# Linear attention and top-1 experts on one core: attention steps regrouped by array shape, scores as 64x64 products, first loads by half heads, early places for four chunks, a fixed load order

## The chip, the cores and the metric

The kernel runs on one core of a Trainium2 chip. The core has a matrix engine (TensorE, "PE" in the profile, its weight loads "PEld"), a vector engine (VectorE, "DVE"), a scalar engine (ScalarE, "ACT"), a general one (GpSimd, "POOL") and one that mostly issues transfers (SyncE, "SP"). They run side by side, each through its own queue in order, and wait for each other through semaphores. Transfers between the device memory (DRAM) and the on-chip memory (SBUF) run on 16 DMA engines; they are issued from the queues of SP, ACT or POOL. PE's products land in PSUM, eight banks of 128 partitions x 512 numbers of 4 bytes. All data are 32-bit floats.

The metric is the device time of one execution in microseconds (us). Before the change the median of 10 runs is 477.11 us (476.78 to 479.06).

## The reference: what is computed

Two parts in a row. First linear attention with a decay: 4 batches, 8 heads, 768 positions, 64 numbers a head. In blocks of 64 positions (the kernel uses blocks of 128, which gives the same sums):

```python
intra = np.einsum('bhic,bhjc->bhij', qb, kb) * Dmask[None]
intra = np.einsum('bhij,bhjd->bhid', intra, vb)
inter = np.einsum('bhid,bhde->bhie', qb * lam_pow[None], kv_state)
out[:, :, sl] = intra + inter
kv_state = lam_block[None, :, None, None] * kv_state + np.einsum('bhsd,bhse->bhde', kb_dec, vb)
```

`Dmask[i, j]` is lam to the power i - j for j up to i, zero beyond; lam is one number a head. Then each of the 3072 output rows of 512 numbers (4 x 768 tokens) goes through one of 8 experts, the one with the highest gate logit:

```python
expert_idx = np.argmax(logits, axis=1)          # logits = x @ w_gate
h = np.maximum(xe @ w1[e], 0.0)                 # 512 -> 1024, for the rows xe of expert e
out[mask] = gate_w[mask, None] * (h @ w2[e])    # 1024 -> 512
```

## The kernel before, in words

**Attention steps.** The positions are cut into 6 chunks of 128 (n), the batches taken in 2 pairs (b): 12 steps, numbered 0 to 11 below, in the list `order` (L699). PE's work of a step is written out by hand, and `pin` (L204) keeps each of its instructions in program order. The other engines' instructions are placed by a scheduler: it takes those that are ready in its own model of time, earlier lines first. Within a step, and for the pair two batches of one chunk:

- `turn_q` and `turn_k` (L216, L228) transpose q and k of the *next* step on PE in two halves of four heads (s = 0, 1), four 128x128 transposes each. ACT copies the results to SBUF as qT and kT, DVE writes qsT, which is q times a decay, and POOL writes kd, which is k times a decay (L238, two buffers).
- `attend_states` (L265) multiplies qsT with the state `st`: 16 products in two groups of 8 ("ways"), which write other halves of the output banks 6 and 7. Between the two an ACT copy of a few numbers (`fence`, L280) makes the second way wait for the first.
- `grow` (L296) makes the state's growth, 32 products kd x v into bank 4. `update` (L308) adds it on DVE to the decayed state, which POOL has put into `sd` (L316).
- `attend` (L282) makes 32 products of v with the masked scores `mt`, into banks 6 and 7.
- `to_sbuf` (L290) copies these two banks on ACT to xT.
- `score` (L243) makes the next step's scores: 32 products of 64x128 (64 rows of the array, 128 columns, 128 wide) into banks 0 to 3, and multiplies them on DVE with the decay mask, giving mt (L254).
- `leave` (L668) and `rows` (L320), in the next step, turn xT back to rows on PE (banks 4 to 7, with the gate's logits in 8 further columns). ACT copies the rows to x and the logits to lg, and issues the transfer of x to `xs` in DRAM.

PE's shapes in a step are 128x128 (leave, turns), 64x64 (states), 128x64 (grow, attend), 64x64 (states) and 64x128 (scores): five, the next step's leave closing the circle.

**Routing.** When a group of chunks is complete, `choose` (L338) finds on DVE each token's expert and its running counts. A step later `put` (L370) makes the token's place in its expert's list: a product with a triangular matrix (`rank`, bank 5), four small DVE operations, and one indirect transfer from POOL for each chunk. A group is the 4 chunks of one n for n = 0 to 3, and two chunks after that (L641). The group (4, [0, 1]) is called `early`: after it `start_early` (L685) reads how many tokens expert 0 has so far, fetches its first 256 rows (pass "0a"), and later tokens of expert 0 are placed behind them.

**Experts.** Nine passes ("0a", "0b" and one for each other expert), in order of their counts. A pass gathers its rows, transposes them (`turn`, L460), makes the hidden layer (`hidden`, L470, or in seven products for eight, `hidden_fast`), the outputs, and scatters them. The hidden layer of "0a" is begun while the last places are still being made (L778).

**Loads.** `load` (L89) fetches q, k and v of a pair of batches, 512 KB each, with three buffers for each of the three. Entering the next step issues the load for two steps beyond it. The first pair comes in halves by batch, k's through ACT's queue; lam comes behind q on SP's queue, and the gate weights come on ACT's in four transfers (L123). The scheduler may swap loads on SP's queue. The weights of expert 0 (two of 2 MB) are issued from step 9's `enter` (L651).

## Time and profile before

| what | value |
|---|---|
| median of 10 runs | 477.11 us |
| the profiled execution, its time | 477.9 us |
| its span, first to last instruction | 476.1 us |
| granted PE clock, mean | 0.996 |
| PE / PEld busy | 457.8 / 383.7 us |
| DVE / ACT / POOL busy | 224.4 / 126.9 / 247.7 us |
| DMA moved | 72.84 MB, mean 153 GB/s |
| one attention step (51.17 to 60.98) | 9.81 us |
| one attention step with `rank` (60.98 to 71.16) | 10.18 us |
| attention ends, last state products | 128.32 us |
| hidden layer of "0a" ends | 146.91 us |

Read it so: the span is the profiled execution of all the work, and what lies around it adds 1.8 us to give that execution's own time. PE is busy nearly all of it, but the ends of its products are modelled, so its busy time does not tell whether the products were as close as they could be; the starts in the timeline do. The attention part is the first 128 us, and up to 119 us the DMA engines are busy in nine tenths or more of the time as well. After 136 us PE's timeline shows one dense run of expert work up to the end. "L248" is line 248 of the kernel; a row's last bracket says how long the engine had been idle before it and what ended that.

### The profile page before, as it was taken

To read this page: it belongs to the slowest core of one execution; us is meant where nothing else is said; L and a number is where in the kernel's file an instruction comes from. 1 tells how busy PE (TensorE), PEld (TensorE's weight loads), DVE (VectorE), ACT (ScalarE), POOL (GpSimd) and SP (SyncE) were. 2 spreads that over 40 slices of the span, in tenths; PEclk is the share of its full clock that TensorE was granted. 3 is DMA by queue.
4 is the path that set the end of the run, shared out by engine and by line. 5 is a ranking of instruction groups with operands and counts; after the bars stand their busy time and mean duration, and the time that the engine had idled before them with its cause. 6 is when DMAs were issued, how large, how long until landed. Compare 5 with 4: busy or idle time off the path is not lost.

```text
span 476.1 us, 8695 instructions
## 1 busy us (share of the span) xinstructions
PE 457.8 (96%) x3468; PEld 383.7 (81%) x3468; DVE 224.4 (47%) x525; ACT 126.9 (27%) x323; POOL 247.7 (52%) x189
## 2 busy tenths in 40 slices
PE   4899999999999999999999999999999999999994
PEld 3789999998785677957994898699699689779973
DVE  2657758585540134462345437434534623753421
ACT  3364445554320111212121122113112212211310
POOL 5423644524335829849807951991794497711001
PEclk9999999999999999999999999999999999999998
DMA  9999999998219556060606153351633615001001
GB/s 173 238 244 269 228 235 233 281 271 271 90 48 344 149 201 237 24 248 29 220 1 243 48 202 103 140 202 44 244 121 122 241 35 209 0 19 44 1 17 51
DMA packets 99857, 72.84 MB, mean 153 GB/s; under 512 B 81227, under 2 KB 81231, under 8 KB 99809
## 3 DMA queue, kind: packets, MB, share of 16 engines
q1 hardware_dynamic: 88688, 51.97, 39.6%
q0 software_dynamic: 5008, 13.41, 7.8%
q10 hardware_dynamic: 6112, 6.83, 4.7%
q8 instruction: 29, 0.48, 0.4%
q14 instruction: 20, 0.16, 0.1%
HBM read 59.13 MB, written 13.40 MB: 152 GB/s over the span
## 4 chain that ended last, share of the span: by engine, by line
PE 91%; DMA 3%; SPq 2%; DVE 1%; ACT 1%; ACTq 0%; issue 0%; POOLq 0%; POOL 0%
PE p L551 28%; PE p L579 18%; PE po L609 16%; PE ph L475 5%; PE sp L248 4%; PE op L284 4%; PE tp L465 3%; PE tx L326 2%; PE op L272 2%; PE cp L301 2%; PE tx L328 2%; DMA k_in<-in_k_dram 2%; PE tk L213 2%; PE tq L213 2%; SPq L96 2%; DMA back<-in_moe_w_gate_dram 1%
## 5 line engine op out<-in xcount | busy, mean ns | idle before, releaser
L609 PE MATMUL po<-w2t,hT 128*128 128x512 f32 (+2 forms) x224 | 81.1, 597 | 0.0
L436 POOL DMA_INDIRECT xg<-xs,list x24 | 26.0, 1084 | 75.7 <-PE tp L465 70.2
L609 PEld LDWEIGHTS po<-w2t,hT 128*128 128x128 f32 (+2 forms) x224 | 31.6, 169 | 37.5 <-issue 37.2
L562 ACT ACTIVATE hT<-hT 128x384 f32<-128x384 f32 (+2 forms) x56 | 30.2, 538 | 89.8 <-DVE hT L560 89.8
L442 POOL DMA_INDIRECT out_dram<-o,list x24 | 23.7, 990 | 52.0 <-DVE o L615 28.9
L390 POOL DMA_INDIRECT slots<-entry,slot_i x24 | 23.7, 986 | 38.2 <-DVE slot_i L388 14.1
L551 PE MATMUL p<-xgT,w1t 128*128 128x192 f32 (+2 forms) x224 | 42.8, 334 | 0.0
L551 PEld LDWEIGHTS p<-xgT,w1t 128*128 128x128 f32 x224 | 38.7, 190 | 1.1 <-issue 0.8
L238 POOL TENSOR_TENSOR kd<-k_in,kdec 128x512 f32<-128x512 f32 x20 | 20.5, 1044 | 26.5 <-PE cp L301 14.8
L254 DVE TENSOR_TENSOR mt<-sp,decay 128x512 f32<-128x512 f32 x48 | 29.8, 682 | 7.2 <-PE sp L248 7.1
L591 DVE SCALAR_TENSOR_TENSOR o<-p,list,o 128x256 f32<-128x256 f32 x28 | 13.5, 484 | 32.9 <-PE p L579 17.0
L579 PE MATMUL p<-w2t,hT 128*128 128x256 f32 x112 | 26.8, 382 | 0.0
L579 PEld LDWEIGHTS p<-w2t,hT 128*128 128x128 f32 x112 | 21.0, 190 | 6.9 <-issue 4.4
L248 PE MATMUL sp<-qT,kT 64*128 64x128 f32 x384 | 25.1, 281 | 0.0
L248 PEld LDWEIGHTS sp<-qT,kT 64*128 64x128 f32 x384 | 22.8, 191 | 2.2 <-issue 1.9
L284 PE MATMUL op<-mt,v_in 128*64 128x128 f32 x384 | 23.6, 274 | 0.7 <-ACT fence L280 0.7
L475 PE MATMUL ph<-xgT,w1t 128*128 128x256 f32 (+1 forms) x128 | 23.9, 342 | 0.0
L560 DVE TENSOR_TENSOR hT<-p,u_qsT 128x384 f32<-128x384 f32 (+2 forms) x28 | 16.1, 575 | 16.5 <-PE p L551 16.5
L213 PE MATMUL tq<-ident,q_in 128*128 128x128 f32 x96 | 15.4, 286 | 7.5 <-DMA q_in<-in_q_dram 7.5
L284 PEld LDWEIGHTS op<-mt,v_in 128*64 128x64 f32 x384 | 20.7, 137 | 1.5 <-ACT fence L280 1.2
L488 DVE TENSOR_TENSOR u_kT<-p,u_qT 128x384 f32<-128x384 f32 (+2 forms) x14 | 8.1, 577 | 29.3 <-PE p L551 29.3
L293 ACT COPY xT<-op 128x512 f32<-128x512 f32 x24 | 12.9, 589 | 33.6 <-PE op L272 29.8
(162 smaller groups left out, 960.9 us busy)
## 6 DMA issues: line engine op xcount, KB each, us to landing
w1t<-in_moe_w_dram SPq DMA_DIRECT2D x8, 2048.0 KB, 7.9
w2t<-in_moe_w_dram SPq DMA_DIRECT2D x8, 2048.0 KB, 8.9
xs<-x ACTq DMA_DIRECT2D x24, 256.0 KB, 4.3
q_in<-in_q_dram SPq DMA_DIRECT2D x11, 512.0 KB, 8.3
k_in<-in_k_dram SPq DMA_DIRECT2D x11, 512.0 KB, 8.4
v_in<-in_v_dram SPq DMA_DIRECT2D x11, 512.0 KB, 8.8
q_in<-in_q_dram SPq DMA_DIRECT2D x2, 256.0 KB, 3.9
k_in<-in_k_dram ACTq DMA_DIRECT2D x2, 256.0 KB, 5.5
```

What stands on the lines that cost most here:

```text
L213: pin(nc.tensor.transpose(t[:, i, b, :], src[:, b, h:h + 2, :], ident))
L248: pin(nc.tensor.matmul(sp[u][:, i, b, :], lhsT=m.kT[s][halves[u], i, b, :], rhs=m.qT[s][halves[u], i, b, :], start=(i == 0 and b == 0), st ...
L254: nc.vector.tensor_mul(mt[:, u], sp[u], decay[:, u, s * HP // 2:(s + 1) * HP // 2].unsqueeze(2).to_broadcast(shp))
L284: pin(nc.tensor.matmul(out_at(m, b, u, hp), lhsT=m.v[:, b, 2 * hp + u, :], rhs=m.mt[hp // 2][:, u, hp % 2, b, :], start=(m.n == 0 and hp = ...
L390: put = nc.gpsimd.indirect_dma_start(out=slots, out_offset=bass.IndirectOffsetOnAxis(ap=slot_i[:, i:i + 1], axis=0), in_=entry[:, n, b, :] ...
L436: nc.gpsimd.indirect_dma_start(out=dst, out_offset=None, in_=xs[:rows, :], in_offset=bass.IndirectOffsetOnAxis(ap=idx, axis=0))
L442: put = nc.gpsimd.indirect_dma_start(out=out, out_offset=bass.IndirectOffsetOnAxis(ap=idx, axis=0), in_=src, in_offset=None, bounds_check= ...
L475: nc.tensor.matmul(ph, lhsT=w1t[:, dc, fc * P:(fc + 1) * P], rhs=m.xgT[:, dc, :], start=(dc == 0), stop=(dc == DC - 1))
L551: nc.tensor.matmul(p[:, i, :], lhsT=lhs[:, dc, (c + i) * P:(c + i + 1) * P], rhs=rhs[:, dc, :], start=(dc == 0), stop=(dc == DH - 1))
L562: nc.scalar.activation(outs[i][k], outs[i][k], ACT.Relu)
L579: nc.tensor.matmul(p, lhsT=lhs[:, fc, :], rhs=rhs[:, fc, :], start=(fc == 0), stop=(fc == FC // 2 - 1))
L609: nc.tensor.matmul(po[part], lhsT=m.hT[:, fc, t * P:t * P + w], rhs=w2t[:, fc, :], start=(i < k), stop=(i >= FC - k), skip_group_check=True)
```

## The change

- `score` makes 64 products of 64x64 instead of 32 of 64x128: the columns (keys) are split in halves. The masks move to a function of their own, `mask`.
- A step's order becomes: for each half s, turns of the next step's q and k and the rows of one batch of the step before (`leave` is now called for one batch); places; growth; attention with mt; first way of states; scores of the next step and the masks of its first half; second way of states; xT and update; masks of the second half. PE's shapes are then 128x128, 128x64 and 64x64. The first step has an order of its own, and the last one puts the transposes of the early tokens and the places of group (5, [0, 1]) before its second way of states.
- `attend` now opens the accumulation in banks 6 and 7; the second way takes the batches in the other order; the fence copies two numbers on 128 partitions from one bank.
- The decayed state `sd` is issued on POOL at the head of `grow` instead of in `update`.
- The first pair's q and k come in eight transfers of 128 KB (half of the heads of one batch), q's on SP and k's on ACT; v comes in one. lam and the four gate transfers go to POOL's queue.
- Loads on SP's queue keep program order (`in_order`, the former `pin`), and the weights of expert 0 are issued ahead of the very last v.
- The groups of four chunks run to n = 4, and `early` is the group of n = 3, so the 256 early rows are found among the first 16 chunks instead of 18.
- The first 128 hidden columns of "0a" are made in fixed order ahead of the last step's rows, the rest behind.

```diff
     def load(n, b0, first=False):
         got = [qkv.tile([P, 2, H, D], F32, tag=name, name=f"{name}_in") for name in "qkv"]
-        per = 1 if first else 2
-        for t, src in zip(got, (q, k, v)):
-            queue = nc.scalar if first and src is k else nc.sync
-            for b in range(0, 2, per):
-                queue.dma_start(
-                    out=t[:, b:b + per].rearrange("p b h d -> p (b h) d"),
-                    in_=src[b0 + b:b0 + b + per, :, n * C:(n + 1) * C, :].rearrange(
-                        "b h s d -> s (b h) d"))
-            if first and src is q:
-                load_lam()
+        where = slice(n * C, (n + 1) * C)
+        if first:
+            for hs, b, i in itertools.product((slice(0, HP), slice(HP, H)), range(2), range(2)):
+                (nc.sync, nc.scalar)[i].dma_start(
+                    out=got[i][:, b, hs],
+                    in_=(q, k)[i][b0 + b, hs, where, :].rearrange("h s d -> s h d"))
+        for i, src in enumerate((q, k, v)):
+            if (n, b0) == (NSTEP - 1, B - 2) and src is v:
+                weights.append(load_weights(0))
+            if not first or src is v:
+                in_order(nc.sync.dma_start(
+                    out=got[i].rearrange("p b h d -> p (b h) d"),
+                    in_=src[b0:b0 + 2, :, where, :].rearrange("b h s d -> s (b h) d")))
         return got
...
+    nc.gpsimd.dma_start(out=lam_bc, in_=lam.partition_broadcast(P))
     loaded = {(0, 0): load(0, 0, True), (0, 2): load(0, 2)}
...
     by_chunk = moe_w_gate.rearrange("(c j u d) e -> j u d c e", c=DC // 2, j=2, u=2)
     for j, u in itertools.product(range(2), range(2)):
-        nc.scalar.dma_start(out=back[(u ^ j) * D:((u ^ j) + 1) * D, :, P + j * E:P + (j + 1) * E],
+        nc.gpsimd.dma_start(out=back[(u ^ j) * D:((u ^ j) + 1) * D, :, P + j * E:P + (j + 1) * E],
                             in_=by_chunk[j, u])
     before = const.tile([P, P], F32, name="before")
     make_upper_triangular(nc, before, val=1.0, diag=False)
...
     def load_weights(e):
         w1t = wpool.tile([P, DC, F], F32, tag="w1", name="w1t")
-        nc.sync.dma_start(out=w1t, in_=pick(w1_r, e))
+        in_order(nc.sync.dma_start(out=w1t, in_=pick(w1_r, e)))
         w2t = wpool.tile([P, FC, MD], F32, tag="w2", name="w2t")
-        nc.sync.dma_start(out=w2t, in_=pick(w2_r, e))
+        in_order(nc.sync.dma_start(out=w2t, in_=pick(w2_r, e)))
         return w1t, w2t
     weights = []
...
-        for i, b, u in itertools.product(range(HP // 2), range(2), range(2)):
-            pin(nc.tensor.matmul(
-                sp[u][:, i, b, :], lhsT=m.kT[s][halves[u], i, b, :], rhs=m.qT[s][halves[u], i, b, :],
+        for i, b, u, keys in itertools.product(range(HP // 2), range(2), range(2), halves):
+            in_order(nc.tensor.matmul(
+                sp[u][keys, i, b, :], lhsT=m.kT[s][halves[u], i, b, keys],
+                rhs=m.qT[s][halves[u], i, b, :],
...
+        m.sp.append(sp)
+    def mask(m, s):
+        shp = [P, HP // 2, 2, C]
         mt = work.tile([P, 2, HP // 2, 2, C], F32, tag="mt", name="mt")
         for u in range(2):
             nc.vector.tensor_mul(
-                mt[:, u], sp[u],
+                mt[:, u], m.sp[s][u],
                 decay[:, u, s * HP // 2:(s + 1) * HP // 2].unsqueeze(2).to_broadcast(shp))
         m.mt.append(mt)
-    fence = const.tile([P, 1], F32, name="fence")
+    fence = const.tile([P, 2], F32, name="fence")
...
+    def attend(m):
+        m.op = [bank(6 + b, [P, HP, C], f"op{b}") for b in range(2)]
+        for hp, b, u in itertools.product(range(HP), range(2), range(2)):
+            in_order(nc.tensor.matmul(
+                out_at(m, b, u, hp), lhsT=m.v[:, b, 2 * hp + u, :],
+                rhs=m.mt[hp // 2][:, u, hp % 2, b, :],
+                start=(hp == 0), stop=(m.n == 0 and hp == HP - 1), skip_group_check=True))
     def attend_states(m, way):
-        if way == 0:
-            m.op = [bank(6 + b, [P, HP, C], f"op{b}") for b in range(2)]
         if m.n > 0:
-            for hp, b in itertools.product(range(HP), range(2)):
+            for hp, b in itertools.product(range(HP), (1, 0) if way else (0, 1)):
                 u = b ^ way
-                pin(nc.tensor.matmul(
+                in_order(nc.tensor.matmul(
...
-                    start=(way == 0 and hp < 2), stop=(way == 1 and hp >= HP - 2),
-                    skip_group_check=True))
+                    start=False, stop=(way == 1 and hp >= HP - 2), skip_group_check=True))
         if m.n > 0 and way == 0:
-            nc.scalar.copy(fence[halves[0]], out_at(m, 1, 1, HP - 1)[:, C - 1:])
-    def attend(m):
-        for hp, b, u in itertools.product(range(HP), range(2), range(2)):
...
+            nc.scalar.copy(fence, m.op[1][:, 0:HP:HP - 1, C - 1])
...
     def grow(m):
+        if 0 < m.n < NSTEP - 1:
+            shp = [P, 2, HP, D]
+            m.sd = work.tile(shp, F32, tag="sd", name="sd")
+            nc.gpsimd.tensor_tensor(out=m.sd, in0=st[:, m.b:m.b + 2],
+                                    in1=sdec.unsqueeze(1).to_broadcast(shp), op=ALU.mult)
         if m.n < NSTEP - 1:
             m.cp = bank(4, [P, 2, HP, D], "cp")
...
             else:
-                shp = [P, 2, HP, D]
-                sd = work.tile(shp, F32, tag="sd", name="sd")
-                nc.gpsimd.tensor_tensor(out=sd, in0=to,
-                                        in1=sdec.unsqueeze(1).to_broadcast(shp), op=ALU.mult)
-                nc.vector.tensor_add(to, m.cp, sd)
+                nc.vector.tensor_add(to, m.cp, m.sd)
...
-    def hidden(m, w1t):
...
-        for fc in range(FC):
+    def hidden(m, w1t, fcs=range(FC), in_order=lambda inst: inst):
+        if fcs[0] == 0:
+            m.hT = ffn.tile([P, FC, m.n], F32, tag="hT", name="hT", bufs=1)
+        for fc in fcs:
...
                         in_=empty.rearrange("p r c -> p (r c)").bitcast(F32))
     nc.gpsimd.dma_start(out=xs[0, :].rearrange("(c p) -> c p", c=DC), in_=zeros[:DC, :])
-    groups = ([(n, list(range(B))) for n in range(NSTEP - 2)]
-              + [(n, [b, b + 1]) for n in range(NSTEP - 2, NSTEP) for b in range(0, B, 2)])
-    early = groups[NSTEP - 2]
+    groups = ([(n, list(range(B))) for n in range(NSTEP - 1)]
+              + [(NSTEP - 1, [b, b + 1]) for b in range(0, B, 2)])
+    early = groups[NSTEP - 3]
     group_of = {(n, b): (n, bs) for n, bs in groups for b in bs}
     lgs = {}
     base = [ebase]
...
-        if (n, b) == (NSTEP - 2, B - 2):
-            weights.append(load_weights(0))
...
-        for s, turn_one in (((0, turn_q), (1, turn_q), (0, turn_k), (1, turn_k)) if not (n or b)
-                            else ((0, turn_q), (0, turn_k), (1, turn_q), (1, turn_k))):
-            turn_one(m, s)
...
-    def leave(m):
-        for b in range(2):
-            n, bs = group_of[m.n, m.b + b]
...
-            rows(m, b, lgs[0][:, i])
...
+    def leave(m, b):
+        n, bs = group_of[m.n, m.b + b]
...
+        rows(m, b, lgs[0][:, i])
...
-        fetch(m, 1 + ((NSTEP - 2) * B + CUT) * C)
+        fetch(m, 1 + (NSTEP - 2) * B * C)
...
     cur, last = enter(*order[0]), None
     for s in range(2):
+        turn_q(cur, s)
+        turn_k(cur, s)
         score(cur, s)
+        mask(cur, s)
     for i in range(len(order)):
         due = chosen.pop() if chosen else None
-        if last:
-            leave(last)
         ahead = enter(*order[i + 1]) if i + 1 < len(order) else None
-        if due:
-            give_places(due)
+        if i == 0:
+            grow(cur)
+            for s in range(2):
+                turn_q(ahead, s)
+            attend(cur)
+            update(cur)
+            to_sbuf(cur)
+            later_decays()
+            for s in range(2):
+                turn_k(ahead, s)
+        else:
+            for s in range(2):
+                if ahead:
+                    turn_q(ahead, s)
+                    turn_k(ahead, s)
+                leave(last, s)
+            if due:
+                give_places(due)
+            grow(cur)
+            attend(cur)
         attend_states(cur, 0)
-        grow(cur)
-        attend(cur)
-        if chosen and chosen[0][:2] == early:
-            give_places(chosen.pop())
-        attend_states(cur, 1)
-        to_sbuf(cur)
-        update(cur)
-        if i == 0:
-            later_decays()
         if ahead:
             for s in range(2):
                 score(ahead, s)
+            mask(ahead, 0)
+        else:
+            turn(passes[0], in_order)
+            give_places(chosen.pop())
+        attend_states(cur, 1)
+        if i > 0:
+            to_sbuf(cur)
+            update(cur)
+        if ahead:
+            mask(ahead, 1)
         last, cur = cur, ahead
-    turn(passes[0], pin)
-    give_places(chosen.pop())
-    leave(last)
+    hidden(passes[0], weights[0][0], range(1), in_order)
+    for b in range(2):
+        leave(last, b)
     give_places(chosen.pop())
...
     for i, m in enumerate(passes):
         w1t, w2t = weights[max(i - 1, 0)]
         if i < 2:
-            hidden(m, w1t)
+            hidden(m, w1t, range(i == 0, FC))
         else:
             w1, w2 = w1_next, w2_next
             hidden_fast(m, w1)
```

## Prediction

> **What bounds the kernel now.** First the page's shares, its slices and its chain: TensorE (PE) is on 91% of the chain that ends last, so a saving counts only if PE reaches its last product sooner.
>
> ```profile
> span 476.1 us, 8695 instructions
> PE 457.8 (96%) x3468; PEld 383.7 (81%) x3468; DVE 224.4 (47%) x525; ACT 126.9 (27%) x323; POOL 247.7 (52%) x189
> DMA  9999999998219556060606153351633615001001
> PE 91%; DMA 3%; SPq 2%; DVE 1%; ACT 1%; ACTq 0%; issue 0%; POOLq 0%; POOL 0%
> ```
>
> Then PE's timeline of one attention step, and its weight loads in the same stretch. A step runs from 51.17 to 60.98 in the chain (9.81 us), one with the rank products (0.37) to 71.16 (10.18).
>
> ```profile
> 54.90 0.67 PE L272 MATMUL op<-qsT,st 64*64 64x128 f32 x16
> 55.50 1.15 PE L301 MATMUL cp<-v_in,kd 128*64 128x64 f32 x32
> 56.48 1.92 PE L284 MATMUL op<-mt,v_in 128*64 128x128 f32 x32
> 58.33 0.67 PE L272 MATMUL op<-qsT,st 64*64 64x128 f32 x16
> 58.92 2.06 PE L248 MATMUL sp<-qT,kT 64*128 64x128 f32 x32
> ...
> 60.91 0.50 PE L326 MATMUL tx<-back,xT 128*128 128x136 f32 x2
> ```
>
> ```profile
> 54.90 0.43 PEld L272 LDWEIGHTS op<-qsT,st 64*64 64x64 f32 x16 [0.17 <-issue]
> 55.49 1.01 PEld L301 LDWEIGHTS cp<-v_in,kd 128*64 128x64 f32 x32 [0.17 <-issue]
> 56.42 1.73 PEld L284 LDWEIGHTS op<-mt,v_in 128*64 128x64 f32 x32
> 58.33 0.43 PEld L272 LDWEIGHTS op<-qsT,st 64*64 64x64 f32 x16 [0.17 <-issue]
> ```
>
> PE never rests, but where the array shape changes the next weights come 0.17 late; where it stays (L301 to L284) they don't. A step changes shape five times.
>
> Third, the start. The loads saturate the DMA engines for 119 us, and PE waits for the third pair's k.
>
> ```profile
> 7.28 1.76 PE L213 MATMUL tq<-ident,q_in 128*128 128x128 f32 x7 [2.07 <-DMA q_in<-in_q_dram]
> 8.82 1.92 PE L213 MATMUL tk<-ident,k_in 128*128 128x128 f32 x8
> ...
> 24.87 0.63 PE L213 MATMUL tk<-ident,k_in 128*128 128x128 f32 x4 [0.30 <-DMA k_in<-in_k_dram]
> ```
>
> Last, the two engines that could become late: POOL's multiplications hold back DVE's small operations (two stretch from 0.17 to a microsecond).
>
> ```profile
> 56.40 0.99 DVE L367 TENSOR_TENSOR acc<-acc,oh 128x8 f32<-128x8 f32 x1
> 57.42 0.97 DVE L366 COPY ohc<-acc 128x8 f32<-128x8 f32 x1
> ```
>
> ```profile
> 56.33 2.04 POOL L238 TENSOR_TENSOR kd<-k_in,kdec 128x512 f32<-128x512 f32 x2 [2.03 <-issue]
> ```
>
> **The step in new order.** Turns and rows, then growth and attention (128x64), then states, scores, states (64x64): three shapes. Scores become 64 products of 64x64 for 32 of 64x128. The nearest row is the state products' (same shape and width): 16 take 0.60 in the chain, switch included, and singly read their sets of four start 0.109 apart, so 64 take 16 x 0.109 = 1.74; if every 16 cost 0.60, 2.40. I take 1.74, since no switch lies inside; today's scores take 1.99. From chain durations: turns 1.75, rows 2.05, growth 1.08, attention 1.75, states 0.60 (switch included), scores 1.74, states 0.44: 9.41 against 9.81. Over steps 2 to 8 (31.19 to 100.95): 7 x 0.40 = 2.8 saved.
>
> The Trainium skill ("TensorE: Matmul & The Clock Gate", "Wait — 56ns, not 53.3ns?") has a 62 ns floor per product with one decoding path; by that 64 would take 4.0 and each step lose 1.9. The state rows (0.60/16 = 38 ns) deny that floor here.
>
> **What becomes late.** (a) Rows now follow after two turns (0.87) instead of the scores (1.99) that covered the xT copies; the first copy ends about 0.9 after the last state product's start, the rows come at 1.07: free by 0.1, and what it would hold up is everything, since PE's order is fixed. The growth bank's update (0.69 on DVE) ends at 1.02 too: free. (b) Attention writes the banks from which ACT copies x, now with only the growth (1.08) between, where turns (1.75) were. ACT's own row (two xT at 0.48, four qT/kT at 0.48, three lg/x pairs at 0.33, an issue 0.33) ends near 5.0 after the step's start, attention is ready at 4.9: 0 to 0.3 in steps without rank. (c) In these steps (2, 4, 6, 8) choose's 16 DVE operations start near 4.8, and two kd run on POOL just then, after the growth that frees their buffers: two operations go by till 6.9, fourteen more at 0.14 end near 9.0. The masks should start at 8.4, so they are up to 0.6 late. Behind them on DVE stand the update and the masks of the second half; the next turns on PE need their banks, and the rows the update's, so part of the lateness lands on PE at the head of the next step. (b) and (c) together: 0 to 0.8 a step of this kind; nothing if the scheduler sets the masks ahead of choose's tail. I take 0.28 x 4 = 1.1, the lateness halved, because PE has 0.2 to 0.4 of room before each bank. sd (1.04 on POOL), issued before the growth, fills idle POOL time: nothing, unless it too runs beside choose; then DVE is a third microsecond late. The fence (0.16 on ACT) is covered by the scores (1.74); uncovered it cost 0.49 at 117.58. Steps 2 to 8: -1.7 (0 to -2.8).
>
> **The start.** First loads are eight of 128 KB on SP and ACT; lam and the four gate loads go to POOL's queue (five issues at some 0.75, the duration of POOL's own DMA issues at 4.48 and 11.97; POOL's wait of 5.2 before kd at 10.98 hides them, and ident comes 0.75 later, at 2.2, ahead of the first q at 4.6), and ACT loses its 4.55 us of issuing. Half heads let pair 0 turn and score its first half while the second lands, so its scores end before 13.16, by 0 to 3 us. None of that reaches the end, since PE then meets the load stream: in new order the rows of pair 0 wait behind the turn of k of pair 2. That k landed at 24.73. Between 8 and 9 us the DMAs moved 35 GB/s, beside 174 to 249 in the microseconds around; eight loads in flight ahead of v close this hole: 0.9 sooner, 23.85. (Bounds: 24.73, nothing gained; 22.4, if the eight loads of 4.2 MB and slots' 0.43 run without any hole at 240 GB/s, with 1 us for the larger packets.) From there: 0.13 to start, turns 1.31, rows 1.85, growth 1.08, attention 1.75, scores and switch 1.9: 31.87 against 31.19: +0.7 (-0.8 to +1.6). From there the loads run ahead: v was issued at 10.54, 18.90, 27.06 and 35.00, 8.2 us a step, where PE will use one in 9.4 or more. The fixed order can hold SP's queue behind a v that waits for its buffer, with the next q and k behind it, but these are used two steps later and land in 8.3: free. w1 and w2 now stand ahead of the last v, as w1 and w2 largely did (v landed at 117.24); it is needed near 119: free, else 1 for 1.
>
> Another section of that page ("Why this matters for your kernels") speaks against the change: no PE gaps over some 3 us, or the clock halves. The rows above show a slow clock at the start alone: turns 0.213 apart (eight in 1.92, where four later take 0.60), against 0.109 from 11.6 on; 7.28 to 11.6 at half speed lost 2.1. Between the scores of pair 1 (end about 18.5) and 23.85 PE has only four turns; by the rule PE would restart slow. My sum has no loss: the gap before 15.76 (1.3 idle) did not restart it, and the four turns split the wait into halves of some 2.5; the other end is a whole restart, 2.1.
>
> **The tail.** Chain pieces: step 9 11.37 (100.95 to 112.32), step 10 9.59, then to the end of the early hidden layer 25.0 (146.91). New step 9: 9.41, one rank instead of two 0.37, had 0.39 and its wait 0.3: 10.47, -0.9. Step 10 has no growth to cover (b): 9.41 - 1.08 + 0.15 switch + 1.1 wait = 9.58, 0. After it: xT wait 0.98, rows 1.85, rank 0.37, wait and switch 0.5, attention 1.75, states 0.6, turns of the early tokens with switch and copies 1.55, rank 0.37, states 0.6, first hidden block 1.93, rows 1.85, rank and count 0.6, hidden rest 56 x 0.216 = 12.1: 25.05, 0. So -0.85 (-1.7 to +0.8). The early list: the inputs send 259 of the first 2048 tokens to expert 0, so its 256 places fill and no rows are added. The late list ends 1.6 later in relation to PE, but its gather landed at 151.6 and is used at 160.5: covered, else 1 for 1.
>
> **Sum.** +0.7 - 1.7 - 0.85 = -1.85. The profiled execution took 477.9 (span 476.1, 1.8 around it); the median of the ten is 477.11, 0.8 less. 477.11 - 1.85 = 475.3.
>
> **Rivals.** Full saving: masks and banks on time, k at 22.4: -0.8 - 2.8 - 0.85 = -4.4, 472.7; DVE 47% busy speaks for it, the stretched rows against. Eaten: (b) and (c) cost 0.7 in each of four steps, 2.8: +0.7 - 0.85 = 477.0, no change, as if the shapes' gain never appeared. Slower: the wait for pair 2's k alone. If it lands no sooner (+1.6) and PE restarts slow (+2.1): 3.7 - 1.7 - 0.85 = +1.15, 478.3; it decides once the idle makes more than 2.5 there. For it: a saturated queue and 5 idle us; against: the hole at 8 us.
>
> **How the numbers follow.** Forecast 0.48, full 0.17, eaten 0.19, slower 0.16. A measurement tells 0.2%, 0.95 us, from no change. The forecast's own range is 474.0 to 476.5, 0.44 of its 0.48 beyond that bound: with the full case, faster 0.61. Same: the other 0.04 and 0.17 of the eaten case, 0.21. Slower: its rest and the last case, 0.18. The range takes in the other cases' values: 472.5 to 478.5.
>
> **What would show it.** Right: steps of 9.4 and 9.8 to 10.1 in the chain; no 0.17 gap between states and scores; the 64-product scores near 1.75; third k about 24 and PE idle before it. Wrong: scores near 2.4; mask waits ahead of turns in every second step; transposes 0.21 apart after 24 us; waits for lists after 150.

## The result, and the profile after

The changed kernel takes 484.62 us (median of 9 runs, 484.37 to 487.50) beside 477.45 for the kernel before on the same chip (31 runs): a ratio of 1.0158, 95% interval 1.0143 to 1.0173. It is 7.2 us slower; 475.3 was forecast, and 478.5 was the upper end of the range. The profiled execution took 486.88 us (span 485.1, 1.8 around it): its mean clock is 0.993, because of a half-speed stretch at the start. Three of the 9 runs have such a clock (0.992 to 0.994) and take 485.9 to 487.5; the others have 0.996 to 0.998 and 484.4 to 485.2, so the median doesn't hold that stretch. Medians here and below are of all executions; the ratios leave out those over 1.5% above the fastest of the same kernel.

The page of the changed kernel, span, PE's row and the chain:

```profile
span 485.1 us, 9452 instructions
PE 457.8 (94%) x3848; PEld 383.9 (79%) x3848; DVE 224.3 (46%) x512; ACT 128.1 (26%) x322; POOL 250.8 (52%) x194
...
PE 81%; DVE 9%; SPq 3%; ACT 2%; DMA 2%; issue 1%; ACTq 0%; POOLq 0%; POOL 0%
```

PE is busy as long as before (457.8 us) in a span 9 us longer, and VectorE has come onto the chain: 9% for 1%. Where the 9 us are is told by the start of the first attention product of each step:

| us | before | after | difference |
|---|---|---|---|
| attention of step 2 starts | 36.49 | 38.54 | +2.05 |
| from there to attention of step 9 | 70.13 | 77.56 | +7.43 |
| from there to the first product of L609 / L611 | 40.13 | 39.55 | -0.58 |
| from there to the end | 329.3 | 329.4 | +0.1 |

PE's timeline of one new step, with the change in three shapes that was foreseen:

```profile
81.98 1.15 PE L306 MATMUL cp<-v_in,kd 128*64 128x64 f32 x32
82.96 1.92 PE L271 MATMUL op<-mt,v_in 128*64 128x128 f32 x32
84.81 0.67 PE L281 MATMUL op<-qsT,st 64*64 64x128 f32 x16
85.30 1.93 PE L246 MATMUL sp<-qT,kT 64*64 64x128 f32 x64
87.04 0.81 PE L281 MATMUL op<-qsT,st 64*64 64x128 f32 x16
87.78 0.66 PE L211 MATMUL tq<-ident,q_in 128*128 128x128 f32 x4
88.27 0.60 PE L211 MATMUL tk<-ident,k_in 128*128 128x128 f32 x4
89.65 0.47 PE L327 MATMUL tx<-back,xT 128*128 128x136 f32 x2 [0.78 <-DVE st L319]
```

The scores take 87.04 - 85.30 = 1.74 us from start to start, as forecast, and no switch shows around them. The loss is the last line: the rows wait for the update of the states. VectorE's timeline in the same step, and the two rows of the waits:

```profile
86.35 0.17 DVE L367 COPY ohc<-acc 128x8 f32<-128x8 f32 x1
86.43 2.48 DVE L257 TENSOR_TENSOR mt<-sp,decay 128x512 f32<-128x512 f32 x4
88.82 0.68 DVE L319 TENSOR_TENSOR st<-cp,sd 128x512 f32<-128x512 f32 x1
```

```profile
PEld tx L327 <- ACT qT L218: 9.3, 8, 1.4
PE tx L327 <- DVE st L319: 7.6, 8, 1.2
```

All four masks (2.48) stand in VectorE's queue ahead of the update (0.68), although the program writes the second half's masks behind it: the scheduler orders VectorE's work by when it expects it to be ready, and only PE's and SP's orders are fixed. Growth, whose bank the update reads, is long done; the rows reuse that bank, so they wait till 88.82 + 0.68 = 89.50 and start at 89.65. From the end of the first half's scores PE has 0.87 (second half) + 0.74 (states and switch) + 0.87 (turns) of work, VectorE 2.48 + 0.68. It happens in eight steps, with 0.78 to 1.23 us of idle time in each and 7.6 us in all. ScalarE's row (9.3) is the weight load of the same products; it names qT, done at 89.4, and the update ends last.

Last the start. PE's timeline, and the windows of 20 to 24 and 24 to 27.3 us (columns: length; busy and instructions of PE, weight loads, VectorE, ScalarE, POOL; granted clock; DMA share; GB/s):

```profile
21.47 0.63 PE L211 MATMUL tq<-ident,q_in 128*128 128x128 f32 x4 [1.56 <-DMA q_in<-in_q_dram]
24.10 1.09 PE L211 MATMUL tk<-ident,k_in 128*128 128x128 f32 x4 [2.01 <-DMA k_in<-in_k_dram]
24.98 0.66 PE L327 MATMUL tx<-back,xT 128*128 128x136 f32 x2
25.43 0.66 PE L329 MATMUL tx<-back,xT 128*128 128x136 f32 x2
```

```profile
20.00:24.00 4.00, 0.63 (x4) 0.42 (x4) 2.24 (x4) 0.59 (x1) 0.00 (x0) 0.98 0.98 222
24.00:27.30 3.30, 3.20 (x15) 3.23 (x16) 0.00 (x0) 1.29 (x5) 0.00 (x0) 0.51 1.22 223
```

PE worked 0.63 of 4 us, and then for 3.4 us ran at half speed: the pairs of the rows' products start 0.455 apart (24.98, 25.43), where the same pairs start 0.23 apart later (27.90, 28.14).

### The profile page after: what moved, and what is told of

It reads as the page before. It is cut to its first block, busy times and chain, and to the rows that moved or that the text cites. A ratio compares the mean times of both kernels' runs of the same rounds, so it can differ in the third digit from the quotient of the medians.

```text
span 485.1 us, 9452 instructions
## 1 busy us (share of the span) xinstructions
PE 457.8 (94%) x3848; PEld 383.9 (79%) x3848; DVE 224.3 (46%) x512; ACT 128.1 (26%) x322; POOL 250.8 (52%) x194
## 4 chain that ended last, share of the span: by engine, by line
PE 81%; DVE 9%; SPq 3%; ACT 2%; DMA 2%; issue 1%; ACTq 0%; POOLq 0%; POOL 0%
PE p L553 27%; PE p L581 18%; PE po L611 16%; PE ph L477 5%; DVE mt L257 3%; PE tp L466 3%; PE op L271 3%; SPq L104 3%; DMA k_in<-in_k_dram 2%; PE tx L327 2%; PE tx L329 2%; PE sp L246 2%; PE cp L306 1%; DVE st L319 1%; PE op L281 1%
## 5 line engine op out<-in xcount | busy, mean ns | idle before, releaser
L611 PE MATMUL po<-w2t,hT 128*128 128x512 f32 (+2 forms) x224 | 81.1, 597 | 0.0
L611 PEld LDWEIGHTS po<-w2t,hT 128*128 128x128 f32 (+2 forms) x224 | 31.6, 169 | 37.5 <-issue 37.2
L593 DVE SCALAR_TENSOR_TENSOR o<-p,list,o 128x256 f32<-128x256 f32 x28 | 13.5, 484 | 32.9 <-PE p L581 17.0
L327 PE MATMUL tx<-back,xT 128*128 128x136 f32 x96 | 20.2, 293 | 8.3 <-DVE st L319 7.6
L246 PE MATMUL sp<-qT,kT 64*64 64x128 f32 x768 | 24.8, 277 | 2.3 <-ACT kT L230 1.8
L246 PEld LDWEIGHTS sp<-qT,kT 64*64 64x64 f32 x768 | 22.2, 137 | 3.6 <-ACT kT L230 2.7
L222 DVE TENSOR_TENSOR qsT<-tq,qdec 128x512 f32<-128x512 f32 x20 | 13.7, 687 | 21.9 <-ACT qT L218 21.9
L327 PEld LDWEIGHTS tx<-back,xT 128*128 128x128 f32 x96 | 15.1, 196 | 10.3 <-ACT qT L218 9.3
L477 PEld LDWEIGHTS ph<-xgT,w1t 128*128 128x128 f32 x128 | 20.6, 190 | 1.7 <-issue 0.2
```

Of the source, the lines that this page charges most:

```text
L246: in_order(nc.tensor.matmul(sp[u][keys, i, b, :], lhsT=m.kT[s][halves[u], i, b, keys], rhs=m.qT[s][halves[u], i, b, :], start=(i == 0 and ...
L327: in_order(nc.tensor.matmul(flat[:, :W], lhsT=m.xT[b][:, 2 * c, :], rhs=back[:, c, :W], start=True, stop=False, skip_group_check=True))
L477: in_order(nc.tensor.matmul(ph, lhsT=w1t[:, dc, fc * P:(fc + 1) * P], rhs=m.xgT[:, dc, :], start=(dc == 0), stop=(dc == DC - 1)))
L611: nc.tensor.matmul(po[part], lhsT=m.hT[:, fc, t * P:t * P + w], rhs=w2t[:, fc, :], start=(i < k), stop=(i >= FC - k), skip_group_check=True)
```

## The experiments

Chips differ, so each group of runs, all on one chip, has its own runs of the kernel before, and ratios are to these. "2 to 9" is attention of step 2 to attention of step 9 in the profiled execution, as in the table above (before 70.13, after 77.56). Where the size of a gap stands in no row's bracket, it is taken from the start of one product to the start of the next, about 0.3 more than the idle time.

| run | median us | before | ratio, 95% interval | 2 to 9 |
|---|---|---|---|---|
| e1_update_first | 481.50 | 480.57 | 1.0024, 0.9994 to 1.0055 | 71.52 |
| e2_extra_mask | 490.36 | 480.57 | 1.0210, 1.0173 to 1.0247 | 80.88 |
| e3_wide_scores | 486.02 | 480.57 | 1.0127, 1.0092 to 1.0163 | 77.66 |
| e5_rows_first | 485.28 | 480.57 | 1.0110, 1.0081 to 1.0139 | 77.19 |
| e7_both | 497.66 | 487.65 | 1.0212, 1.0173 to 1.0250 | 80.58 |
| e8_both_wide | 499.86 | 487.65 | 1.0251, 1.0216 to 1.0286 | 82.72 |
| e4_narrow_only | 490.58 | 487.65 | 1.0069, 1.0042 to 1.0096 | 76.00 |
| c_after (the changed kernel) | 486.43 | 480.53 | 1.0104, 1.0052 to 1.0156 | 78.07 |
| e7_again | 482.59 | 480.53 | 1.0007, 0.9970 to 1.0045 | 71.35 |
| e8_again | 481.77 | 480.53 | 1.0011, 0.9980 to 1.0042 | 72.68 |
| e4_again | 482.54 | 480.53 | 1.0037, 1.0011 to 1.0064 | 75.32 |
| e10_shift_after | 521.49 | 487.27 | 1.0695, 1.0648 to 1.0741 | 88.20 |
| e6_loads_only | 487.22 | 487.27 | 1.0000, 0.9977 to 1.0022 | 73.40 |
| e1_again | 499.23 | 487.27 | 1.0219, 1.0178 to 1.0259 | 80.41 |
| e11_shift64 | 486.97 | 480.77 | 1.0133, 1.0105 to 1.0160 | 76.92 |
| e12_shift64_first | 482.71 | 480.77 | 1.0036, 1.0003 to 1.0069 | 70.31 |
| c_after2 (the changed kernel) | 485.59 | 480.77 | 1.0097, 1.0065 to 1.0129 | 78.48 |

### Is it the update behind the masks?

One line pinned (e1_update_first): the second half's masks keep their written place behind the update.

```diff
-            nc.vector.tensor_mul(
+            mul = nc.vector.tensor_mul(
                 mt[:, u], m.sp[s][u],
                 ...
+            if s == 1:
+                in_order(mul)
```

> The four scores' masks of a step stand on VectorE in the order first half, update, second half, where the changed kernel has both halves and then the update; nothing else differs. Theory (the update behind the masks is the cause): the eight PE gaps of 1.05 to 1.50 us ahead of the rows shrink to the 0.1 to 0.3 of a weight change, each step loses some 1.0 us, attention of steps 2 to 9 takes about 70 us instead of 77.6, and the time falls by 7 to 8.5, to 476 to 477.5. Rival A (ScalarE's copies of x end as late as the update, so the rows start no earlier): the gaps keep more than half their size, the waits name ScalarE's xT, and the time falls by less than 4. Rival B (VectorE's loop of masks, update and scaled q is as long as the step, whatever its order): the wait moves to the turns of the second half, whose banks the late masks free, and the time falls by less than 3.

VectorE's and PE's timelines of e1_update_first in step 4:

```profile
60.29 1.28 DVE L257 TENSOR_TENSOR mt<-sp,decay 128x512 f32<-128x512 f32 x2
61.50 0.69 DVE L321 TENSOR_TENSOR st<-cp,sd 128x512 f32<-128x512 f32 x1
62.10 1.28 DVE L257 TENSOR_TENSOR mt<-sp,decay 128x512 f32<-128x512 f32 x2
```

```profile
61.29 0.66 PE L211 MATMUL tq<-ident,q_in 128*128 128x128 f32 x4
61.78 0.60 PE L211 MATMUL tk<-ident,k_in 128*128 128x128 f32 x4
62.55 0.47 PE L329 MATMUL tx<-back,xT 128*128 128x136 f32 x2 [0.17 <-ACT xT L295]
```

The eight gaps are gone (0.17 left, now ScalarE's copy of x), and no wait took their place at the second half's turns: rivals A and B fall. Undisturbed steps are 9.55 to 9.56 and 10.13 to 10.22 us. Steps 2 to 9 take 6.0 us less than in the changed kernel, 0.7 short of what the waits promised (7.6 x 7/8 = 6.7); a PE gap of another kind, 1.61 us for 0.83, takes as much, and the fourth part comes to it. The time is 1.0024 of the kernel before, where 1.0158 was on the first chip and 1.0104 and 1.0097 on two others (c_after, c_after2), so by these the edit is worth 0.7 to 1.3%; the forecast of 476 to 477.5 us was made for a chip on which before takes 477.

The opposite edit lengthens the wait (e2_extra_mask), in `mask` behind the first half's masks:

```diff
+        if s == 0 and m.n > 0:
+            extra = work.tile([P, HP // 2, 2, C], F32, tag="extra", name="extra", bufs=1)
+            in_order(nc.vector.tensor_mul(
+                extra, m.sp[s][1],
+                decay[:, 1, s * HP // 2:(s + 1) * HP // 2].unsqueeze(2).to_broadcast(shp)))
```

> The changed kernel with one more mask product of the first half (128x512, 0.62 us on VectorE) into a buffer that nobody reads, right behind the first half's own masks and so ahead of the update; no output depends on it. Theory (the end of the update on VectorE sets each step): each of the eight PE gaps ahead of the rows grows from 1.05-1.50 to 1.65-2.1 us and the time rises by 8 x 0.62 = 5.0, to 489 to 490.5. Rival (PE waits at the rows for something else, and the update only ends at about the same time): a rise of less than 2.5.

VectorE's and PE's rows of e2_extra_mask in a step without ranks:

```profile
78.89 0.68 DVE L262 TENSOR_TENSOR extra<-sp,decay 128x512 f32<-128x512 f32 x1
79.48 1.28 DVE L257 TENSOR_TENSOR mt<-sp,decay 128x512 f32<-128x512 f32 x2
80.68 0.68 DVE L324 TENSOR_TENSOR st<-cp,sd 128x512 f32<-128x512 f32 x1
81.51 0.47 PE L332 MATMUL tx<-back,xT 128*128 128x136 f32 x2 [1.21 <-DVE st L324]
```

From one attention to the next, six of the seven steps 2 to 8 are 0.59 to 0.60 longer than in the changed kernel's trace (11.13 for 10.53 without ranks), for a mask of 0.62; the seventh, from step 5 to 6, holds a gap of another kind in the changed kernel (0.83 at 75.28). The rows still start 0.15 behind the update. The first product of L611 (the end of this stretch) comes at 160.47 for 155.65, 4.8 later; 5.0 was expected. The gaps themselves are 1.48 (1.21 idle), less than expected, because part of the delay now shows ahead of the turn of k (0.86 at 45.36), whose bank the extra product reads. VectorE's end of masks and update sets the step.

The shape alone undone (e3_wide_scores):

```diff
-        for i, b, u, keys in itertools.product(range(HP // 2), range(2), range(2), halves):
+        for i, b, u in itertools.product(range(HP // 2), range(2), range(2)):
             in_order(nc.tensor.matmul(
-                sp[u][keys, i, b, :], lhsT=m.kT[s][halves[u], i, b, keys],
-                rhs=m.qT[s][halves[u], i, b, :],
+                sp[u][:, i, b, :], lhsT=m.kT[s][halves[u], i, b, :], rhs=m.qT[s][halves[u], i, b, :],
```

> The changed kernel with the scores as 32 products of 64x128 instead of 64 of 64x64: the shape part of the change undone. Theory (each step of the changed kernel is as long as the path from the first half's scores over VectorE's masks and update to the rows): only the first half's scores lie on that path, whose 0.87 us become some 1.0, and the second half's longer run is taken out of the gap; per step +0.1 to +0.3 us, in all +1 to +3, 485.5 to 487.5. Rival (PE's own work sets each step): scores of 2.0 instead of 1.75 and two more switches of 0.17, some +0.6 a step, +5 to +7. Second rival (the narrow products are the cause of the loss): the time falls.

Steps of 10.75 for 10.53: +0.22, as for a step set by VectorE; two more switches and 0.25 more of scores would be +0.6 if PE set it. The narrow scores are so not what this step waits for, and of what they save only the part of the first half counts while VectorE sets it. The profile names ScalarE's copy of q (0.74 idle) as what ends the rows' wait here; it ends at 87.97, as the update does (87.29 + 0.68). That the rows don't need this copy is seen in e1_update_first, where it keeps its place and the wait is gone. The changed kernel wasn't among these runs, so the times say nothing finer.

### The start

In the second step of the loop alone the rows come first (e5_rows_first):

```diff
         else:
+            if i == 1:
+                for s in range(2):
+                    leave(last, s)
             for s in range(2):
                 ...
-                leave(last, s)
+                if i > 1:
+                    leave(last, s)
```

> The changed kernel with one thing moved: in the second step of the attention loop alone the rows of the first pair are emitted ahead of the turns of the third, so that PE has 1.85 us of work while the third pair's q and k are still on their way. Theory (PE loses there what it idles, and at times a half-speed stretch behind it): attention of step 2 starts about 1.85 us earlier (near 28.1 instead of 29.9), the clock shows no half-speed stretch at 24 to 27, and the time falls by 1.5 to 2, to 482.6 to 483.1; if the clock falls to half without this change in the timed executions too, by up to 3.5. Rival (the gain is taken back because the later loads or the gaps ahead of the rows set the pace anyway): a fall of less than 0.5.

```profile
24.00:27.30 3.30, 3.30 (x64) 3.13 (x64) 1.42 (x3) 1.56 (x3) 1.24 (x2) 1.00 1.04 284
```

In this window of e5_rows_first the clock is 1.00 where it was 0.51, and attention of step 2 starts at 36.45, 2.1 sooner. Attention of step 1 even starts 3.7 sooner (26.21 for 29.91); a wait of 1.55 for the next pair's k, at 32.18, takes the difference back. The first product of L611 comes 2.5 sooner than in the changed kernel (153.19), so the rest is not swallowed in this trace. The times fall short of the expected 482.6, on a chip where before takes 3.1 us more; without the changed kernel beside it they leave the size open.

The loads of the change alone, in the kernel before (e6_loads_only), that is `load`, the queue of lam and the gate, and the fixed order of loads:

```diff
+        if first:
+            for hs, b, i in itertools.product((slice(0, HP), slice(HP, H)), range(2), range(2)):
+                (nc.sync, nc.scalar)[i].dma_start(...)
+    nc.gpsimd.dma_start(out=lam_bc, in_=lam.partition_broadcast(P))
...
-        nc.scalar.dma_start(out=back[(u ^ j) * D:...
+        nc.gpsimd.dma_start(out=back[(u ^ j) * D:...
```

> The kernel before with the new loads alone: first loads by half heads from two queues, lam and the gate from GpSimd's queue, the later loads in written order. Theory (the eight loads close the hole in the load stream at 8 us): the third pair's k lands 0.5 to 0.9 us sooner than at 24.7, attention of step 2 starts 0.5 to 0.9 us sooner, the steps keep 9.81 and 10.18 us, and the time is 0.997 to 0.999 of the kernel before. Rival (PE meets the load stream later anyway, or a fixed load order holds a load behind one that waits for its buffer): 0.999 to 1.003.

The turn of that k starts at 24.54, and attention of step 2 at 36.16: 0.33 sooner than in the trace of before, and in time nothing that shows (1.0000; the interval is 1 us wide to each side). The hole in the load stream is filled, 218 GB/s between 8 and 9 us where before had 35 (and the changed kernel has 217), but in this trace, from another chip than that of before, the load comes only a third of a microsecond sooner for it.

### Why the mended kernel still isn't faster than before

Both mends together (e7_both), and the same with the scores as in e3 (e8_both_wide); the narrow scores alone in the kernel before (e4_narrow_only), which is e3's diff read backwards.

> The changed kernel with both: the update ahead of the second half's masks, and in the second step of the loop the rows of the first pair ahead of the turns of the third. Theory (two separate losses, at the rows and at the start): the gains add up. The update alone left the kernel at 1.0024 of the kernel before, and the moved rows made attention of step 2 start 2.1 us earlier: 1.0024 - 2.1 / 480 = 0.998, 0.994 to 1.001 of the kernel before; steps of 9.55 and 10.13 us, and one or two PE gaps of 0.8 to 2.2 us with no releaser shown, as each kernel with the narrow scores has had. Rival (the gain at the start is swallowed by waits for loads or by the lists behind): no faster than the update alone, 1.001 to 1.005.

> The same with the scores as 32 products of 64x128 instead of 64 of 64x64. The kernels with the narrow scores had PE gaps of 0.83 to 2.20 us among the score and state products, with nothing that releases them; in each of the five larger ones a 16 KB block of PE's instruction queue landed 1.3 to 1.5 us before PE went on. Theory (the narrow scores run through their instructions faster than these blocks come): with half as many score products there is no such gap over 0.5 us, each step is 0.2 to 0.3 longer (9.75 to 9.85 and 10.2 to 10.4), and the time is that of the narrow kernel of this call plus 12 x 0.25 = 3 minus its gaps (2 to 4): within 1.5 us of it. Rival (the gaps come from the new order or from the loads, not from the narrow products): gaps of 0.8 us or more remain, and the time is 3 us above.

> The kernel before with the narrow scores alone (64 products of 64x64 a step). Theory (a narrow step saves PE what the chain showed, 1.99 against 1.75 us): 12 x 0.24 = 2.9 us less, 0.994 of the kernel before, steps of 9.57 and 9.94 us; each PE gap for a late instruction block, 0 to 2 of them, gives 1 to 2 us back: 0.994 to 0.999. Rival (the waits on VectorE's masks, whose banks the turns need, end later in relation to PE and eat the gain): 0.999 to 1.002, with waits ahead of the turns.

This chip answered another question. The kernel before takes 10 us more on it, and in every second step, while GpSimd issues the four scatters of the lists, PE, VectorE and ScalarE halt together. Timelines of e7_both, PE, then POOL, then VectorE:

```profile
76.05 0.43 PE L283 MATMUL op<-qsT,st 64*64 64x128 f32 x4 [0.15 <-issue]
76.77 0.47 PE L283 MATMUL op<-qsT,st 64*64 64x128 f32 x5 [0.29 <-issue]
77.54 0.45 PE L283 MATMUL op<-qsT,st 64*64 64x128 f32 x4 [0.29 <-issue]
```

```profile
76.05 0.96 POOL L393 DMA_INDIRECT slots<-entry,slot_i  x1 [0.30 <-issue]
77.31 0.96 POOL L393 DMA_INDIRECT slots<-entry,slot_i  x1 [0.30 <-issue]
```

```profile
79.37 0.69 DVE L321 TENSOR_TENSOR st<-cp,sd 128x512 f32<-128x512 f32 x1 [3.23 <-PE tq L211]
```

PE goes on in pieces of three to five products with up to 0.29 us of idle time between them, the update begins 1.1 us after the last scatter was issued, though the states' last product had ended at 78, and ScalarE's copies xT begin at 79.30, after 5.12 idle. So the question stays open on this chip, and the three were run again on another one with the changed kernel beside them.

> The changed kernel itself, on the same chip as the three runs that follow it, since chips differ: on that of the first experiments the kernel before took 480.6 us, on that of the second 487.7, where the first comparison had 477.5. Expected: 1.014 to 1.018 of the kernel before, with eight gaps of 1.05 to 1.5 us ahead of the rows; on a chip on which VectorE and PE see each other's results later, more.

> Update ahead of the second half's masks and rows ahead of the turns in the second step, on another chip. On the last one PE, VectorE and ScalarE each stood still for up to 2 us in every second step while GpSimd issued the four scatters of the lists (the update began at 54.94, 2.1 us behind the last product that it waited for; PE went on in pieces of five products with 0.56 us between); on the chip before that none of this showed. Theory (that belongs to the chip): on a chip where the kernel before takes 477 to 481 us this one takes 0.994 to 1.001 of it, its steps are 9.55 and 10.13 us, and PE gaps with no releaser lie 1.3 to 1.5 us behind the landing of an instruction block. Rival (the new order puts the scatters beside its dense products, and loses there on any chip): 1.01 or more of the kernel before, with gaps in each step that follows a rank step.

> The same with the scores as 32 products of 64x128. Theory (the narrow scores outrun the instruction blocks): no gap over 0.5 us without a releaser between attention of step 2 and the last attention, steps of 9.75 to 9.85 and 10.2 to 10.4 us, the time within 1.5 us of the narrow kernel's. Rival: gaps as in the narrow kernel, the time 2.5 to 3 us above it.

> The kernel before with the narrow scores alone. Theory (the saving of 0.24 us a step is real, and late instruction blocks take part of it): 0.994 to 0.999 of the kernel before. On the last chip it was 1.0069, with gaps at products 345, 1099 and 1729, which are 100 and whole blocks of some 125 products, and more gaps beside the scatters. Rival (the loss there came from the narrow products as such, on any chip): 1.004 or more.

There nothing of the standstills shows. With both mends the kernel takes 1.0007 of before and by the ratios 4.7 us less than the changed kernel on this chip; steps 2 to 9 are 6.7 us shorter and attention of step 2 is 1.7 sooner, but the stretch from attention of step 9 to L611 is 42.90 for 39.55. There one PE gap of 1.66 without a releaser is followed by 0.94 of waiting for ScalarE, and the clock record has a half-speed stretch at 125.8 to 129.2. With the wide scores the clock stays full and the gaps are smaller, but two are left (0.65 at 90.68, 1.09 at 115.08), not none: the expectation holds only in part. The steps are 9.96 and 10.31, longer than the 9.81 and 10.18 of before: with wide scores the new order has five shapes again. The narrow scores alone shorten the steps of before to 9.57 and 9.94, exactly as priced, and the kernel is 0.4% slower all the same. Its trace has a gap of 2.52 ahead of the rows at 83.51 and one of 0.85 at 106.59, one of 2.54 at 99.65, where ScalarE's row names the landing of a load of v, and a half-speed stretch at 16.9 to 20.3. The row at 83.51 names VectorE's masks, but these had ended at 83.03, and a step later the rows start at 93.52 while the masks run on to 95.23.

### What those gaps are

They come back at the same place of the program on different chips, at different times: product 1099 (the changed kernel, c_after, e4_narrow_only), 1347 to 1352 (e1, e2, e5, c_after, c_after2, e4_again), 1727 to 1729 (e2, c_after, c_after2, both of e4), 2095 or 2096 (e1, e7_again). These lie 2, 3 and 3 times some 125 apart (e7_again has two more, at 1720 and 1843), and in the trace's transfers 16 KB of PE's instructions are fetched about once per 125 products and their weight loads. The changed kernel's page has this queue (transfers, MB, share of 16 engines) as

```profile
q8 instruction: 32, 0.52, 0.5%
```

Two attempts to shift the stream against the program by extra products misjudged their price: 64 products of 8 columns (e9_shift, 511.6 us in one run) and 62 of 64x64x128 in one quarter of the array (e10_shift_after).

> The changed kernel with the update ahead of the second half's masks, and 64 small products (64x8, of constants, into a bank nobody reads) while PE waits for the third pair's k: everything behind them stands 64 products later in PE's instruction stream. In three kernels a PE gap with no releaser lay at product 1347, 1350 and 1351 of the program, at 82, 86 and 91 us; others at 1099, 1727 and 2096, which are 2, 3 and 6 times some 125 products away, and 125 products with their weight loads are one 16 KB block of instructions. Theory (PE waits for such a block at its border): the gaps stay on that lattice counted with the 64, so that in the program they lie 64 products earlier (near 1035, 1160, 1286, 1411, 1536, 1662, 1787, 1912, 2037) or vanish where that is not in a dense stretch; none is at 1347 to 1351 or at 2096. Rival (a place in the program or a load stops PE): a gap again within 10 products of 1350 or of 2096, counted without the 64. The small products take some 2 us of a wait of 4, so that the time is that of the kernel without them within 1 us, gaps apart, and the clock shows no half-speed stretch at 24 us.

> The changed kernel with 62 more products of 64x64x128 on constants, into a bank nobody reads, while PE waits for the third pair's k (2.1 to 2.3 us; at 0.027 us each they take 1.7): all later work stands 62 products, half an instruction block, further back in PE's stream. In the changed kernel, on two chips, PE gaps with no releaser lie at products 1099, 1351 and 1727 (351 does not count: PE waits there for other things). Theory (PE waits at the border of an instruction block): no such gap within 10 of those places of the program (counted without the 62); new ones, if any, at 1037, 1163, 1289, 1414, 1540, 1665, 1790, 1915 or 2035 of the program, within 6. Rival (a place in the program, a load or a scatter stops PE): gaps again at 1099, 1351 or 1727. The clock shows no half-speed stretch at 24 us, so that the time is 0 to 2 us under the changed kernel's.

Each product of the program is two in the profile (the 32 that `score` emits for a step are its 64), so these were 128 and 124 by the profile's count, a whole block, and they took 10.8 and 13.7 us. Both also met chips with the standstills: e9's gaps lie at the places of e7_both's, e10's at those of the run below, next to the scatters. A shift by a whole block can't tell a place in the program from a border; but these gaps come every four to six products (1863, 1869, 1873 of e1_again), not every 125.

> The changed kernel with the update ahead of the second half's masks, beside the changed kernel with 62 more products on the same chip, so that the price of the update's place is had without a change of chip. Theory: 5 to 8 us less than the changed kernel (1.010 to 1.016 of the kernel before), so 0.998 to 1.004; no gap ahead of the rows over 0.45 us between attention of steps 2 and 9, steps of 9.55 and 10.2, and PE gaps at 1347 to 1352, 1727 or 2095 that take the rest. Rival (the gaps ahead of the rows were worth less than their sum, since other waits step in): less than 4 us under it.

On that chip 1.0219, and steps of 12.6 to 14.3 beside the scatters: no answer on the update. The next attempt repeats real score products, 64 as the profile counts them, in all four quarters, in the changed kernel (e11) and in e1 (e12):

```diff
                     turn_q(ahead, s)
+                    if (i, s) == (1, 0):
+                        spare = [bank(4 + u, [P, HP // 2, 2, C], "spare") for u in range(2)]
+                        for t, j, b, u, keys in itertools.product(
+                                range(2), range(HP // 2), range(2), range(2), halves):
+                            in_order(nc.tensor.matmul(
+                                spare[u][keys, j, b, :], lhsT=cur.kT[0][halves[u], j, b, keys],
+                                rhs=cur.qT[0][halves[u], j, b, :], start=True, stop=True,
+                                skip_group_check=True))
                     turn_k(ahead, s)
```

> The changed kernel with one half's scores computed twice more (64 products as the profile counts them, 1.75 us at the price of the real ones) into two banks nobody reads, while PE waits 2.1 to 2.3 us for the third pair's k: all later work stands 64 products, half an instruction block of some 125, further back in PE's stream. The changed kernel on two chips has PE gaps without a releaser at products 1099, 1351 and 1727. Theory (PE waits at the border of an instruction block): none within 10 of those places of the program, counted without the 64; new ones, where there are any, near 1035, 1161, 1287, 1412, 1538, 1663, 1789, 1914 of the program. Rival (a place in the program, a load, a scatter): gaps again at 1099, 1351 or 1727. The clock shows no half-speed stretch at 24 us, so that the time is 0 to 2 us under the changed kernel's of this call. On a chip where PE goes in pieces beside GpSimd's scatters, as on that where the kernel before took 487 us, this can't be read.

> The same 64 more products in the kernel with the update ahead of the second half's masks, whose gaps lay at products 345, 1347, 2095 and 2096. Theory (block borders): none within 10 of 1347 or 2096 of the program, but near 1035, 1161, 1287, 1412, 1538, 1663, 1789, 1914 or 2039. Rival (the program's place): again at 1347 or 2096. Against the kernel without the update's move: 5 to 8 us less.

> The changed kernel on the same chip, so that the two runs before are read against it: 1.010 to 1.016 of the kernel before, gaps at 1099, 1351 or 1727 if the chip is like the first and the third.

PE's timelines of c_after2 and of e11_shift64 at their gaps:

```profile
88.11 0.32 PE L281 MATMUL op<-qsT,st 64*64 64x128 f32 x1 [1.04 <-issue]
...
110.61 0.66 PE L281 MATMUL op<-qsT,st 64*64 64x128 f32 x13 [1.91 <-issue]
```

```profile
76.50 0.38 PE L211 MATMUL tq<-ident,q_in 128*128 128x128 f32 x2 [0.41 <-issue]
...
120.34 0.34 PE L246 MATMUL sp<-qT,kT 64*64 64x128 f32 x4 [1.32 <-issue]
```

The control's gaps are at 1351 and 1727 again. With 64 products ahead none is there: e11's are at 1162 and 1915 of the program (1161 and 1914 were named beforehand), which are 1226 and 1979 of the stream, 125 before 1351 and 252 (two blocks) behind 1727. e12's are at 848, 1972 and 2096 of the stream (784, 1908 and 2032 of the program); 2096 is where e1 had its gap, now with other products in it. In c_after2, e11 and e12 PE goes on 1.2 to 1.5 us after a block's transfer has ended (in c_after2 at 86.84 and 109.12, in e11 at 75.08 and 118.82). So PE waits here for its next block of instructions: the gaps move with the stream, and each ends behind a landing. Why a block comes too late is not shown: most borders pass without a gap, and nearly all gaps are within or just behind the states, scores and states (192 instructions in some 3 us). e11 runs at full clock at 24 us, and isn't faster for it (486.97 beside 485.59): its gap of 1.59 falls behind attention of step 9, and the stretch from there to L611 is 40.85 for 39.54.

On this chip the update's place is worth 4.7 us by the ratios (e11 against e12), 6.6 in steps 2 to 9 of their traces. No version with the new order beats the kernel before: the two nearest, 1.0007 and 1.0011, can't be told from it.

## Why the prediction was wrong

**The step that failed** is the sentence under (a): "The growth bank's update (0.69 on DVE) ends at 1.02 too: free." It puts the update where it stood before, right behind the last state products. In the new order VectorE has the next pair's masks to do just then, and the written order, first half, update, second half, which (c) takes for VectorE's queue, isn't its order: all four masks come first. In the step shown the update ends at 89.50, 1.97 after the last state product's start (87.53) for the 1.02 of the sum, and the rows start 2.12 after it for 1.07. PE's idle time for it is 7.6 us over eight steps, 6.7 of them in steps 2 to 8, where the sum has nothing. With this order alone undone (e1) these waits go; with one more mask ahead of the update (e2) the steps grow by 0.60 for its 0.62.

**The other terms.** Steps 2 to 8 were to take 70.13 - 1.7 = 68.4. With the update in place and one block gap of 0.97 taken off, e12 takes 69.3: the rest is the rows' wait for ScalarE's copy of x, "free by 0.1" in (a), which takes 0.14 in each of seven steps (9.55 for 9.41). (b) and (c) were given 1.1: in e1 attention doesn't wait for ScalarE in these steps, and steps with ranks are 0.57 to 0.66 longer for 0.45 of products, so 0.1 to 0.2 each. VectorE's small operations do stretch beside kd (0.94 and 0.74 in the changed kernel), and the masks follow them at once.

**Right**: the narrow scores at 1.74, not 2.40 (sets of four start 0.109 apart, 27 ns a product); no switch among the 64x64 products; the tail, -0.85 forecast, -0.58 measured; k of the third pair, 23.85 forecast, landed at 23.97. The 62 ns a product that the Trainium skill ("TensorE: Matmul & The Clock Gate", "Wait — 56ns, not 53.3ns?") gives for one of two ways of decoding doesn't bind here either (0.027 us measured).

**Mis-sized**: the start, +0.7 forecast, +2.05 in the profiled execution. The sum ended at 31.87 with the scores and the profile ended them at 33.67; 1.7 of this is the half-speed stretch, which the prediction gave a whole restart (2.1) as its other end and took at nothing. The same page's section "Why this matters for your kernels" asks for no PE gap over some 3 us; neither gap here is as long, yet its warning was nearer than my argument that four turns split the wait. The profiled execution shows the half-speed stretch behind gaps of 1.8 and 2.3 with four products between, and e5 and e11, which fill that wait, have full clock there. In two thirds of the timed runs it doesn't happen, so the median owes it little: without it the start is +0.35, and +0.35 + 7.43 - 0.58 = +7.2, the measured loss on this chip.

**Not in the prediction at all**: the instruction blocks, 0.83 us in the profiled execution and up to 4 where the wait for VectorE no longer hides them. The narrow scores, right in price, don't pay on their own (1.0037): in that trace the gaps at block borders (2.52 and 0.85) come to the 2.9 that twelve steps save, and the wait for ScalarE and the half-speed stretch stand beside them; what each is worth in the median is not shown.

**The rivals**: the slower case (478.3) came from the start alone; its clock restart appeared, and it wasn't the loss. No rival had VectorE's queue order in it, although the prediction named the update and the masks as standing on one engine.

## What to carry to other kernels

Where a change moves one engine's products to another place in a fixed order, write down the neighbouring engine's whole queue at the new place, in the order in which the scheduler will put it, before any of its operations is called free; a written order holds only where it is pinned. A saving in product time counts only while the instructions for it arrive: halving products in size doubles the instructions of the stretch, and that price shows as gaps with no releaser at regular product numbers. A gap that one wait has hidden shows up when that wait is mended, so a mend is worth less than the wait it removes.

## What the runs showed of the hardware that was not expected

- PE stops at some borders of its instruction blocks: gaps of 0.55 to 2.5 us from start to start, some 125 products (with their weight loads) apart or multiples of it, ending 1.2 to 1.7 us behind the landing of 16 KB. The wide scores in the new order have them too (e8_again, 1213 and 1586).
- The clock fell though PE was busy throughout, with small products. In e9_shift PE ran 64x8 products back to back from 22.95 (0.057 us each), and the windows show a clock of 0.50 from 26.6; in e10_shift_after 13.5 us of 64x128 products in the same place kept 1.00:

```profile
22.90:26.60 3.70, 3.70 (x65) 3.65 (x63) 1.77 (x3) 0.59 (x1) 0.00 (x0) 1.00 1.26 224
26.60:33.70 7.10, 7.10 (x69) 7.08 (x67) 0.00 (x0) 0.00 (x0) 0.00 (x0) 0.50 1.09 218
```

- Products of 64x64 in one quarter of the array take 0.110 us each (124 in 13.7, e10_shift_after), those that go round all four 0.027.
- On the chips of two of the six groups of runs (e7_both's and e10_shift_after's) PE, VectorE and ScalarE halt beside GpSimd's scatters, and the kernel before takes 487.3 to 487.7 us instead of 477.5 to 480.8. The new order with one or both mends, whose dense products lie beside the scatters, loses 2.1 to 2.5% there (e7_both, e8_both_wide, e1_again). What differs in these chips stays open.
